# Earlier mixing, reading back and turning of token rows in four groups, and a sign strip of raw weight words moved to ScalarE

## The chip, the core and the metric

The kernel runs on one core of a Trainium2 chip. The metric is the device time of one launch in microseconds; of the kernel before, three runs are shown. The profile is one further execution of the same program, taken by the hardware profiler.

## The reference

Three stages feed each other: a causal retention layer over 4 x 576 tokens (8 heads of 64), a mixture of 8 experts of which each token uses two, and a dense layer with a gated activation. Cut to what matters:

```python
ret = (q @ k.T / 8) * Dmat          # decayed, causal; x = ret @ v, 2304 rows of 512
logits = x @ w_gate + log1p(exp(x @ w_noise)) * noise
top2, weights = two best experts of each row, softmax of the two
out[rows of e] += weight * (relu(x[rows of e] @ w1[e]) @ w2[e])      # 8 experts, 512 -> 1024 -> 512
h = out @ w_in                                                       # 512 -> 2048
y = (h * clip(h + 3, 0, 6) / 6) @ w_out                              # 2048 -> 512
```

The two matrices of the last layer arrive as 64-bit floats, and the kernel turns them into 32-bit floats itself. Each 32-bit operand of a big product is split into a high and a low part, so that every product is three passes on TensorE.

## The kernel before

The program is written out by hand: every engine (TensorE, VectorE, ScalarE, GpSimd, and the DMA queue of SyncE) works through its own list in the order in which the Python code issues it, and waits where a semaphore says so. Nothing is reordered by a scheduler.

**The expert stage** (`moe`) is ten sweeps. A sweep has eight steps f = 0 to 7, one for each 128 hidden columns. In the six middle sweeps a step has two runs of rows: 360 rows in three tiles ("ga" in PSUM) and 256 rows in two ("gb"). A step issues the first product for both runs (`g1`, L683, 12 matmuls each), the Relu and the low part of its result (L735 on ScalarE, L736 on VectorE), up to two splits of coming weights (`wstep`, L544 on ScalarE and L545 on VectorE), and then the second product of the step before (`flush`, `g2`, L694, 15 matmuls). "ga" is one PSUM buffer, so the g1 of the next step can start only when L736 has read it. Late in a sweep, `x_tile` turns the rows of the next sweep: `turn` transposes 32 x 32 blocks on VectorE (L636), copies the high part on ScalarE (L638) and takes the low part on VectorE (L639).

**The conversion of the 64-bit weights** fills the gaps of the same sweeps. There are 64 pieces of 128 x 256 words. `CV = (2, 2, 2, 1, 1, 1, 1, 1)` says how many pieces a step takes, so the first three steps of a sweep are double steps. For a piece, `cv_load` reads the raw words (SyncE), `cv_run` computes on VectorE and stores through SyncE later (`cv_store`, L594):

```python
v.tensor_scalar(a, hi, 0x7FFFFFFF, None, op0=OP.bitwise_and)      # L578, strip the sign
v.tensor_scalar(a..., min, max)                                   # L579, clamp
v.tensor_scalar(a, a, 3, 0x3FFFFFF8, shift, and)                  # L580
v.scalar_tensor_tensor(t, hi, -0x40000000, a, and, or)            # L582
v.tensor_scalar(a, t, -0x800000, None, and)                       # L583, exponent
nc.scalar.activation(lf, lo, AF.Copy, scale=2.0 ** -52)           # L585
nc.gpsimd.tensor_mul(lf, lf, a); nc.gpsimd.tensor_add(lf, t, lf)  # L586, L587
```

The tile `a` has two buffers, `lf` three; L585 waits for the store of the piece three before it.

**The dense stage** (`moe2`) works on seven groups of tiles, `GR`: three of 2 tiles, four of 3. A group has 16 steps; a step is `g1` (12 matmuls, "ga" and "gb" in turn), the gated activation (`glu`: L869, L870, L871, L872 between ScalarE and VectorE), and the `g2` of the step before. While a group runs, `x2_prep` makes the input of the next one: it gathers two rows per token from DRAM (GpSimd, L808), mixes them with the two gate weights (L816 on ScalarE, L817 on VectorE), stores the mixed rows (GpSimd's queue, L834), reads them back in blocks (SyncE, four DMAs, L628), and turns them (L636, L638, L639). It is called at the end of step f with the number f - 1, and a table of four numbers says at which number each of these happens: tile j is gathered at j * step, and mixed, read back and turned `mix`, `get` and `cut` later.

Of the kernel before, what the change touches and what calls it, by code (L numbers as in the profile page):

```python
# [7 lines left out]
F32 = mybir.dt.float32  # L8
F32R = mybir.dt.float32r
BF = mybir.dt.bfloat16  # L10
I32 = mybir.dt.int32
U32 = mybir.dt.uint32
AF = mybir.ActivationFunctionType
OP = mybir.AluOpType
# [18 lines left out]
P = 128  # L33
# [31 lines left out]
class K:  # L65
# [482 lines left out]

    def cv_init(self):
        self.cvn, self.cvl = 0, 0  # L550
        self.cvr, self.cvo = {}, []

    def cv_at(self, n, wi, wo):
        p, r = divmod(n, 8)
# [5 lines left out]
    def cv_load(self):  # L560
# [6 lines left out]
        self.nc.sync.dma_start(raw.rearrange("p f w -> p (f w)").bitcast(mybir.dt.int64), src)  # L567
        self.cvr[n] = raw

    def cv_run(self):  # L570
        n, nc, v = self.cvn, self.nc, self.nc.vector
        if not self.f64 or n >= self.cvl:
            return
        self.cvn += 1
        raw = self.cvr.pop(n)
        lo, hi = raw[:, :, 0], raw[:, :, 1]
        a = self.sb.tile([P, 256], I32, name="cva", bufs=2)
        v.tensor_scalar(a, hi, 0x7FFFFFFF, None, op0=OP.bitwise_and)  # L578
        v.tensor_scalar(a.bitcast(F32), a.bitcast(F32), fbits(0x47EFFFFF), fbits(0x38000000), op0=OP.min, op1=OP.max)  # L579
        v.tensor_scalar(a, a, 3, 0x3FFFFFF8, op0=OP.logical_shift_left, op1=OP.bitwise_and)  # L580
        t = self.sb.tile([P, 256], I32, name="cvt", bufs=2)
        v.scalar_tensor_tensor(t, hi, -0x40000000, a, op0=OP.bitwise_and, op1=OP.bitwise_or)  # L582
        v.tensor_scalar(a, t, -0x800000, None, op0=OP.bitwise_and)  # L583
        lf = self.sb.tile([P, 256], F32, name="cvl", bufs=3)
        nc.scalar.activation(lf, lo.bitcast(U32), AF.Copy, scale=2.0 ** -52)  # L585
        nc.gpsimd.tensor_mul(lf, lf, a.bitcast(F32))  # L586
        nc.gpsimd.tensor_add(lf, t.bitcast(F32), lf)  # L587
        self.cvo.append((n, lf))

# [116 lines left out]
    def moe(self, xs0):  # L706
        nc = self.nc
        xs = {(0, 0): xs0}
        self.prev = None
        for si, sw in enumerate(self.SW):  # L710
            nxt = self.SW[si + 1] if si + 1 < len(self.SW) else []
            todo = [(e, r, j) for e, r in nxt for j in range((3, 2)[r])]
            get = list(todo)
            e = sw[0][0]
            accs = None
            for f in range(8):
                n = e * 4 + f // 2
                cur = e * 4 if si in (0, len(self.SW) - 2) else n
                if f % 2 == 0:
                    if self.wsp <= cur + 4:  # L720
                        self.w_split()
                if f % 2 == 0 and (si, f) != (0, 6) or (si, f) == (0, 7):
                    self.w_load()
                self.wstep(0, n)
                if (si, f) == (0, 7):
                    for s in todo:
                        self.x_fin(*s)
                tf = 3 if si == 1 or len(todo) > 3 else 4
                w, fi = self.w[n], f % 2
                subs = []  # L730
                for q, (_, r) in enumerate(sw):
                    c = (NA, NB)[r]
                    hh, hl = self.hid([P, c]), self.hid([P, c])
                    p = self.g1(w, fi, xs[sw[q]], c, "ga" if (r == 0) == (f % 2 == 0 or len(sw) == 2) else "gb")
                    nc.scalar.activation(hh, p, AF.Relu)  # L735
                    nc.vector.scalar_tensor_tensor(hl, p, 0.0, hh.bitcast(F32), op0=OP.max, op1=OP.subtract)  # L736
                    subs.append((hh, hl, (RA, RB)[r]))
                if si == 0:
                    self.rstep()
                    self.send()  # L740
                    if f == 7:
                        for s in todo:
                            self.x_tile(s[0], xs[s[:2]], s[2], "acc", s[1])
                self.wstep()
                self.flush()
                self.wstep()
                if accs is None:
                    accs = [[self.pacc([P, DM]) for _ in range(self.run_of(*s)[1])] for s in sw]
                self.prev = (w, fi, [(*s, a) for s, a in zip(subs, accs)], f == 0, f == 7)
                self.fin = (self.y_out, sw, accs)  # L750

                if si == 0:
                    for _ in range(3):
                        self.rstep()
                        self.send()
                    if f == 4:
                        while self.sent < NT or self.live:
                            self.rstep()
                            self.send()
                        self.count()  # L760
                g = 4 if si == 0 else 0
                if f == g:
                    for s in nxt:
                        if si == 0:
                            self.x_load(*s)
                        xs[s] = self.x_new(s[1])
                    if si < 2:
                        self.fill(range(2, E) if si else range(1, 2))
                if si and get:
                    ee, rr, j = get.pop(0)  # L770
                    self.x_load(ee, rr, [j])
                sub = None
                if si and f >= tf and todo:
                    ee, rr, j = todo.pop(0)
                    sub = self.x_tile(ee, xs[ee, rr], j, r=rr)
                if si > 1:
                    for _ in range(CV[f]):
                        self.cv_run()
                        self.cv_load()
                        self.cv_store()  # L780
                elif si and f > 4:
                    self.cv_load()
                if sub:
                    sub()
                if si == len(self.SW) - 1:
                    self.x2_prep(0, f - 1)
            for s in sw:
                xs.pop(s)
# [30 lines left out]
    def x2_prep(self, gi, f):  # L819

        if gi >= len(self.GR) or f < 0:
            return
        t0, G = self.GR[gi]
        if f == 0:
            self.ys = {}
            self.x2 = (self.act_t([P, 4, 384]), self.act_t([P, 4, 384]))
        step, mix, get, cut = ((0, 2, 4, 5), (3, 5, 8, 11), (3, 5, 8, 11), (2, 5, 7, 10), (3, 3, 5, 7))[min(gi, 4)]
        for j in range(G):
            rows = self.x2d[(t0 + j) * P:(t0 + j + 1) * P]
            if f == j * step:  # L830
                self.ys[j] = self.x2_gather(t0 + j)
            if f == j * step + mix:
                self.x2_mix(t0 + j, self.ys[j])
                self.nc.gpsimd.dma_start(rows, self.ys[j][0])  # L834
            if f == j * step + get:
                self.ys[j] = self.x_blocks(rows)
            if f == j * step + cut:
                c = slice(j * P, (j + 1) * P)
                self.turn(self.ys.pop(j), slice(0, P), self.x2[0][:, :, c], self.x2[1][:, :, c])()
# [193 lines left out]
def fbits(b):  # L1033
    return float(np.array([b], np.uint32).view(np.float32)[0])
# [53 lines left out]
```

## Time and profile before

| | |
|---|---|
| three runs | 986.38, 987.69, 988.9 us; median 987.69 |
| the profiled execution, its own time | 984.52 us |
| its span, first to last instruction | 982.4 us, 16434 instructions |
| TensorE matmul / weight load busy | 960.7 us (98%) / 856.0 us (87%) |
| VectorE / ScalarE / GpSimd busy | 555.3 (57%) / 407.2 (41%) / 203.5 us (21%) |
| mean granted TensorE clock | 0.992 |
| HBM | 97.90 MB read, 39.71 MB written |

The busy share of TensorE leaves 21.7 us of the span in which it ran no matmul. Only what shortens those, or shortens the matmuls that start late because a weight load was held up, can shorten this kernel. The shares of the other engines are averages over stages that differ: the expert sweeps load VectorE far more than the dense groups do.

### The profile page before, as it was taken

To read this page: it belongs to the slowest core of one execution; us is meant where nothing else is said; L and a number is where in the kernel's file an instruction comes from. 1 tells how busy PE (TensorE), PEld (TensorE's weight loads), DVE (VectorE), ACT (ScalarE), POOL (GpSimd) and SP (SyncE) were. 2 spreads that over 40 slices of the span, in tenths; PEclk is the share of its full clock that TensorE was granted. 3 is DMA by queue.
4 is the path that set the end of the run, shared out by engine and by line. 5 is a ranking of instruction groups with operands and counts; after the bars stand their busy time and mean duration, and the time that the engine had idled before them with its cause. 6 is when DMAs were issued, how large, how long until landed. Compare 5 with 4: busy or idle time off the path is not lost.

```text
span 982.4 us, 16434 instructions
## 1 busy us (share of the span) xinstructions
PE 960.7 (98%) x6056; PEld 856.0 (87%) x6056; DVE 555.3 (57%) x1283; ACT 407.2 (41%) x844; POOL 203.5 (21%) x277
## 2 busy tenths in 40 slices
PE   8999899999999999999999999999999999999997
PEld 6888788888888889888889898989899999999996
DVE  5688745777869778786843574343434334334222
ACT  4667424444453353535342473333423333333322
POOL 1246341232314132232400211020112011020000
PEclk9999799999999999999999999999999999999999
DMA  9674747775747576584342742131223012020000
GB/s 342 236 272 168 256 149 227 238 236 166 229 165 220 187 219 188 185 252 156 90 145 70 245 162 84 36 94 43 65 65 86 33 54 76 33 86 23 33 1 36
DMA packets 106183, 138.79 MB, mean 141 GB/s; under 512 B 10469, under 2 KB 66533, under 8 KB 106093
## 3 DMA queue, kind: packets, MB, share of 16 engines
q1 hardware_dynamic: 97821, 111.03, 35.8%
q0 software_dynamic: 7984, 26.10, 7.8%
q8 instruction: 49, 0.80, 0.3%
q10 hardware_dynamic: 288, 0.52, 0.1%
q14 instruction: 41, 0.34, 0.1%
HBM read 97.90 MB, written 39.71 MB: 140 GB/s over the span
## 4 chain that ended last, share of the span: by engine, by line
PE 93%; DVE 4%; issue 1%; ACT 1%; DVEq 0%; ACTq 0%
PE p L694 41%; PE ga L683 22%; PE gb L683 20%; PE sc L192 2%; PE px L214 2%; PE p L175 2%; PE px L204 1%; DVE b L545 1%; PE p L253 1%; DVE xp L636 1%; PE p L238 1%; PE p L112 1%; PE p L272 1%; PE p L264 0%; DVE b L639 0%
## 5 line engine op out<-in xcount | busy, mean ns | idle before, releaser
L694 PE MATMUL p<-b,h 128*128 128x512 f32 (+1 forms) x1824 | 451.6, 393 | 0.0
L694 PEld LDWEIGHTS p<-b,h 128*128 128x128 f32 (+1 forms) x1824 | 330.0, 186 | 65.4 <-DVE h L736 0.3
L683 PE MATMUL ga<-x,b 128*128 128x360 f32 (+2 forms) x1344 | 236.6, 325 | 8.4 <-ACT x L638 5.4
L683 PEld LDWEIGHTS ga<-x,b 128*128 128x128 f32 x1344 | 220.6, 190 | 23.4 <-DVE h L736 8.1
L683 PE MATMUL gb<-x,b 128*128 128x384 f32 (+2 forms) x768 | 129.3, 317 | 0.0
L683 PEld LDWEIGHTS gb<-x,b 128*128 128x128 f32 x768 | 123.3, 190 | 5.2
L545 DVE TENSOR_TENSOR b<-b,b 128x512 fp32r<-128x512 f32 x128 | 93.3, 766 | 9.5 <-ACT b L544 9.3
L586 POOL TENSOR_TENSOR cvl<-cvl,cva 128x256 f32<-128x256 f32 x64 | 47.4, 740 | 241.7 <-ACT h L735 127.6
L683 PE MATMUL gb<-b,b 128*128 128x256 f32 x672 | 90.4, 283 | 0.9 <-DVE b L639 0.9
L872 DVE SCALAR_TENSOR_TENSOR h<-h,h 128x384 fp32r<-128x384 f32 (+1 forms) x112 | 56.2, 502 | 61.1 <-ACT h L871 61.1
L683 PEld LDWEIGHTS gb<-b,b 128*128 128x128 f32 x672 | 87.3, 191 | 2.6 <-DVE b L639 1.9
L871 ACT ACTIVATE h<-h 128x384 fp32r<-128x384 f32 (+1 forms) x112 | 53.7, 479 | 65.3 <-DVE h L870 65.3
L870 DVE SCALAR_TENSOR_TENSOR h<-h,ga 128x384 f32<-128x384 f32 (+1 forms) x56 | 27.8, 497 | 93.5 <-ACT h L869 93.3
L870 DVE SCALAR_TENSOR_TENSOR h<-h,gb 128x384 f32<-128x384 f32 (+1 forms) x56 | 27.8, 497 | 82.9 <-ACT h L869 82.8
L544 ACT ACTIVATE b<-b 128x512 fp32r<-128x512 f32 x128 | 73.9, 625 | 0.0
L869 ACT ACTIVATE h<-ga,three 128x384 f32<-128x384 f32 (+1 forms) x56 | 30.0, 535 | 95.5 <-PE ga L683 95.5
L736 DVE SCALAR_TENSOR_TENSOR h<-gb,h 128x256 fp32r<-128x256 f32 (+1 forms) x64 | 27.7, 433 | 70.7 <-PE p L694 48.2
L834 POOL DMA_DIRECT2D x2d<-s x18 | 10.4, 578 | 267.5 <-DVE s L817 267.4
L869 ACT ACTIVATE h<-gb,three 128x384 f32<-128x384 f32 (+1 forms) x56 | 30.0, 535 | 77.8 <-PE gb L683 77.8
L735 ACT ACTIVATE h<-gb 128x256 fp32r<-128x256 f32 (+1 forms) x64 | 25.3, 396 | 74.9 <-PE gb L683 74.9
L638 ACT ACTIVATE x<-xp 128x512 fp32r<-128x512 f32 (+1 forms) x39 | 22.8, 584 | 80.3 <-DVE xp L636 80.3
L587 POOL TENSOR_TENSOR cvl<-cvt,cvl 128x256 f32<-128x256 f32 x64 | 53.3, 832 | 5.0
(143 smaller groups left out, 891.3 us busy)
## 6 DMA issues: line engine op xcount, KB each, us to landing
b<-in_moe_w_dram SPq DMA_DIRECT2D x64, 512.0 KB, 5.2
s<-xe SPq DMA_DIRECT2D x140, 64.0 KB, 2.9
s<-in_moe_w_in_dram SPq DMA_DIRECT2D x32, 256.0 KB, 3.5
s<-in_moe_w_out_dram SPq DMA_DIRECT2D x32, 256.0 KB, 3.4
yd<-s SPq DMA_DIRECT2D x24, 240.0 KB, 2.5
b<-in_k_dram SPq DMA_DIRECT2D x18, 256.0 KB, 5.3
b<-in_q_dram SPq DMA_DIRECT2D x18, 256.0 KB, 5.4
b<-in_v_dram SPq DMA_DIRECT2D x18, 256.0 KB, 5.3
```

The lines of the kernel that those rows point to most:

```text
L544: self.nc.scalar.activation(h, a, AF.Copy)
L545: self.nc.vector.tensor_sub(l, a, h.bitcast(F32))
L586: nc.gpsimd.tensor_mul(lf, lf, a.bitcast(F32))
L587: nc.gpsimd.tensor_add(lf, t.bitcast(F32), lf)
L683: nc.tensor.matmul(p, a[:, k, f], b[:, k, :n], start=(i == 0), stop=(i == 11))
L694: nc.tensor.matmul(a[:R], x[:, c], y[:, fi, :], start=(first and i == 0), stop=(last and i == 2))
L735: nc.scalar.activation(hh, p, AF.Relu)
L736: nc.vector.scalar_tensor_tensor(hl, p, 0.0, hh.bitcast(F32), op0=OP.max, op1=OP.subtract)
L869: nc.scalar.activation(r, p, AF.Relu, bias=self.three)
L870: nc.vector.scalar_tensor_tensor(r, r, 6.0, p, op0=OP.min, op1=OP.mult)
L871: nc.scalar.activation(gh, r, AF.Copy, scale=1.0 / 6.0)
L872: nc.vector.scalar_tensor_tensor(gl, r, 1.0 / 6.0, gh.bitcast(F32), op0=OP.mult, op1=OP.subtract)
```

## The change

Two parts.

1. In the table of `x2_prep`, the rows for next groups 1 and 2 go from mix 5, get 8, cut 11 to 4, 6, 8, and the row for next group 3 from 5, 7, 10 to 4, 6, 8. The rows for group 0 and for groups 4 to 6 stay.
2. The sign strip of the raw words (L578) leaves VectorE. A new function `cv_abs` does it as an absolute value on ScalarE for the piece after the one just converted. The exponent goes to a tile of its own, `cvs`, with one buffer.

```diff
+    def cv_abs(self):
+        n = self.cvn + len(self.cva)
+        if n in self.cvr:
+            a = self.sb.tile([P, 256], I32, name="cva", bufs=2)
+            self.nc.scalar.activation(a.bitcast(F32), self.cvr[n][:, :, 1].bitcast(F32), AF.Abs)
+            self.cva.append(a)
...
-        a = self.sb.tile([P, 256], I32, name="cva", bufs=2)
-        v.tensor_scalar(a, hi, 0x7FFFFFFF, None, op0=OP.bitwise_and)
+        a = self.cva.pop(0)
...
-        v.tensor_scalar(a, t, -0x800000, None, op0=OP.bitwise_and)
+        s = self.sb.tile([P, 256], I32, name="cvs", bufs=1)
+        v.tensor_scalar(s, t, -0x800000, None, op0=OP.bitwise_and)
...
-        nc.gpsimd.tensor_mul(lf, lf, a.bitcast(F32))
+        nc.gpsimd.tensor_mul(lf, lf, s.bitcast(F32))
...
                         self.cv_run()
                         self.cv_load()
                         self.cv_store()
+                        self.cv_abs()
                 elif si and f > 4:
                     self.cv_load()
+                    if f == 7:
+                        self.cv_abs()
...
-        step, mix, get, cut = ((0, 2, 4, 5), (3, 5, 8, 11), (3, 5, 8, 11), (2, 5, 7, 10), (3, 3, 5, 7))[min(gi, 4)]
+        step, mix, get, cut = ((0, 2, 4, 5), (3, 4, 6, 8), (3, 4, 6, 8), (2, 4, 6, 8), (3, 3, 5, 7))[min(gi, 4)]
```

Where ScalarE's list changes, in a double step of an expert sweep, before (`cvl` is the tile lf, `s` the raw words, the Relus of two steps stand around it):

```order
L735 ACTIVATE h_3236<-ga 128x360
L735 ACTIVATE h_3253<-gb 128x256
L544 ACTIVATE b_3118<-b_2647 128x512
L544 ACTIVATE b_3120<-b_2649 128x512
L585 ACTIVATE cvl<-s_3114 128x256
L585 ACTIVATE cvl<-s_3219 128x256
L735 ACTIVATE h_3330<-ga 128x360
```

And the same step now (lines are 7 higher behind the new function, tile numbers shift):

```order
L742 ACTIVATE h_3251<-ga 128x360
L742 ACTIVATE h_3268<-gb 128x256
L544 ACTIVATE b_3131<-b_2653 128x512
L544 ACTIVATE b_3133<-b_2655 128x512
L592 ACTIVATE cvl<-s_3125 128x256
L574 ACTIVATE cva<-s_3231 128x256
L592 ACTIVATE cvl<-s_3231 128x256
L574 ACTIVATE cva<-s_3246 128x256
L742 ACTIVATE h_3347<-ga 128x360
```

The absolute value of the second piece of the step stands behind the copy L592 of the first one; that of the next step's first piece stands last.

ScalarE's list at the end of the first short dense group, before; `x` is the next group's input, L884 the output of the group that ends:

```order
L869 ACTIVATE h_7535<-gb,three 128x256
L871 ACTIVATE h_7520<-h_7535 128x256
L638 ACTIVATE x_7100<-xp 128x4x128
L869 ACTIVATE h_7565<-ga,three 128x256
L871 ACTIVATE h_7550<-h_7565 128x256
L884 ACTIVATE s_7576<-p_7068 128x512
```

And now:

```order
L645 ACTIVATE x_7164<-xp 128x4x128
L879 ACTIVATE h_7551<-gb,three 128x256
L881 ACTIVATE h_7536<-h_7551 128x256
L879 ACTIVATE h_7577<-ga,three 128x256
L881 ACTIVATE h_7562<-h_7577 128x256
L879 ACTIVATE h_7603<-gb,three 128x256
L881 ACTIVATE h_7588<-h_7603 128x256
L879 ACTIVATE h_7629<-ga,three 128x256
L881 ACTIVATE h_7614<-h_7629 128x256
L894 ACTIVATE s_7640<-p_7132 128x512
```

Three more activations of the old group (L879 with L881) now stand between the last turn and the first activation of the next group.

ScalarE's list in the third short group, which prepares the first group of three tiles, now; L826 is the mix (L816 before):

```order
L645 ACTIVATE x_8132<-xp 128x4x128
L826 ACTIVATE s_8249<-s_8249,gw 128x512
L879 ACTIVATE h_8392<-ga,three 128x256
L881 ACTIVATE h_8377<-h_8392 128x256
```

Here a turn and a mix fall into one step; before, each had a step of its own.

## Rows read from the trace of the kernel before

**Rows 1.** The page: the chain that ended last, by engine.

```profile
PE 93%; DVE 4%; issue 1%; ACT 1%; DVEq 0%; ACTq 0%
```

**Rows 2.** Waits of TensorE (us in total, times, longest); below, who waited for L736.

```profile
PE ga L683 <- ACT x L638: 5.4, 3, 1.8
PE ga L683 <- DVE h L736: 2.4, 1, 2.4
...
  PEld ga L683: 8.1, 19
```

**Rows 3.** Timeline, first short group's end (start us, us, engine, line, [idle before]).

```profile
602.66 0.72 DVE L636 STREAM_TRANSPOSE xp<-s 128x512 f32<-128x512 f32 x1
...
604.92 1.60 PE L683 MATMUL ga<-x,b 128*128 128x256 f32 x12
...
607.74 1.60 PE L683 MATMUL gb<-x,b 128*128 128x256 f32 x12
...
609.18 1.55 PE L694 MATMUL p<-b,h 128*128 128x512 f32 x6
...
611.89 0.60 ACT L638 ACTIVATE x<-xp 128x512 fp32r<-128x512 f32 x1 [1.13 <-DVE xp L636]
...
612.54 1.70 PE L683 MATMUL ga<-x,b 128*128 128x256 f32 x12 [1.80 <-ACT x L638]
```

**Rows 4.** Mix and store there; L834's landing; L628's issue time and landing.

```profile
593.71 0.71 ACT L816 ACTIVATE s<-s,gw 128x512 f32<-128x512 f32 x1
...
595.50 0.57 POOL L834 DMA_DIRECT2D x2d<-s  x1 [6.79 <-DVE s L817]
...
DMA to landing us min/median/max: 2.3/2.5/3.7
...
L628 SPq DMA_DIRECT2D s<-x2d x72: 302/430/593, 552.3 to 891.2; - x72
...
DMA to landing us min/median/max: 1.8/2.8/7.8
```

**Rows 5.** Timeline of the third short group, ScalarE and TensorE.

```profile
689.80 0.47 ACT L869 ACTIVATE h<-ga,three 128x256 f32<-128x256 f32 x1 [1.45 <-PE ga L683]
...
690.77 0.42 ACT L871 ACTIVATE h<-h 128x256 fp32r<-128x256 f32 x1 [0.49 <-DVE h L870]
...
692.43 1.55 PE L694 MATMUL p<-b,h 128*128 128x512 f32 x6
```

**Rows 6.** Instructions of L578 and of L585: ns, min/median/max.

```profile
L578 DVE TENSOR_SCALAR cva<-s x64: 267/280/290, 182.5 to 495.3; 128x256 int32<-128x256 int32 x64
...
L585 ACT ACTIVATE cvl<-s x64: 418/432/447, 181.8 to 495.9; 128x256 f32<-128x256 uint32 x64
```

**Rows 7.** Timeline of an expert sweep, double steps f = 1 and 2, then f = 4.

```profile
299.01 0.44 ACT L585 ACTIVATE cvl<-s 128x256 f32<-128x256 uint32 x1 [1.82 <-issue]
...
301.42 0.47 ACT L735 ACTIVATE h<-ga 128x360 fp32r<-128x360 f32 x1 [0.81 <-DVE cva L578]
...
302.82 0.29 DVE L578 TENSOR_SCALAR cva<-s 128x256 int32<-128x256 int32 x1
...
303.14 0.79 DVE L579 TENSOR_SCALAR cva<-cva 128x256 f32<-128x256 f32 x1
...
305.53 0.52 DVE L736 SCALAR_TENSOR_TENSOR h<-ga,h 128x360 fp32r<-128x360 f32 x1
...
306.11 2.23 PE L683 MATMUL ga<-x,b 128*128 128x360 f32 x12
...
320.08 2.14 PE L683 MATMUL ga<-x,b 128*128 128x360 f32 x12
```

**Rows 8.** Timeline at the start of that sweep; below, who waited for L639.

```profile
287.38 0.68 DVE L639 TENSOR_TENSOR b<-xp,b 128x512 fp32r<-128x512 f32 x1
...
288.12 0.74 PE L683 MATMUL gb<-b,b 128*128 128x256 f32 x4 [0.18 <-DVE b L639]
...
  PEld gb L683: 1.9, 5
```

More of the change, by code (lines that the diff above doesn't have):

```diff
@@ L550, in cv_init @@
         self.cvn, self.cvl = 0, 0
-        self.cvr, self.cvo = {}, []
+        self.cvr, self.cvo, self.cva = {}, [], []
     def cv_at(self, n, wi, wo):
```

## The prediction

> **What bounds the kernel now.** I read four views in this order. The chain of waits says that 93% of the span is TensorE's own work [rows 1], and the table above that it is busy 98% of it: there are 21.7 us without a matmul, part of them in stages that the change does not touch. The waits of TensorE say where the rest is [rows 2]: three waits of 1.8 us for the high part of a turned tile (L638), 5.4 us together, and a family of short ones for L736, of which the matmuls show little (one wait of 2.4 us) but the weight loads 8.1 us in 19 cases. The timeline then shows each place.
>
> The three long waits are the starts of dense groups. At the end of the first short group the last g1 starts at 607.74, the g2 of the step before at 609.18 and lasts 1.55, and then the first g1 of the next group has to wait 1.80 us, until L638 has copied the tile that was turned last [rows 3]. Nothing is missing in DRAM by then: the turn is only the last thing the table orders, at number 14 of 14, behind the whole activation of step 15.
>
> The short ones lie in the expert sweeps, at both ends. In a double step VectorE is behind by half a step; L736 ends at 306.05 and the g1 that overwrites "ga" starts at 306.11 [rows 7]. These 12 matmuls take 2.23 us where the same 12, not held up, take 2.14. At a sweep's start the low part L639 ends at 288.06 and the last four matmuls of "gb" go at 288.12 after a wait of 0.18; five such starts hold the weight loads up by 1.9 us, 0.38 each [rows 8].
>
> **The change part by part.**
>
> *Turns sooner.* No instruction is added or removed; per group 2 or 3 mixes, stores, four-fold reads and turns move. The last turn goes from number 14 to 11 (groups 1 and 2) and to 12 (group 3). A step lasts 604.92 to 607.74, 2.82 us [rows 3], so the copy is done about 8.5 or 5.6 us before the group ends, against a wait of 1.80. Is the data there? From mix to turn the new table leaves 4 steps, 11.3 us. Used are 2.4 us from L816 at 593.71 to the end of L834's issue at 596.07, 2.5 to the store's landing, 4 reads at 0.43 and 2.8 to the last one's landing [rows 4]: 9.4 us, 1.9 to spare. If both DMAs took their longest times, 3.7 and 7.8, the turn would come 4.3 us late, but that is seen once in 18 and once in 140 or fewer; VectorE and ScalarE would stand behind it. SyncE's queue waits for the store inside the reads as it did before; behind them stands only the output of the group that ends. On GpSimd's queue the third tile's gather for group 3 now stands behind the first tile's store, four steps ahead of its mix, and the stores themselves come sooner. I take the whole 5.4 us. The range is 0 (a wait of the same length at another place) to 5.7 (the first 12 matmuls took 1.70 instead of 1.60 [rows 3], three times).
>
> Against it stands one step. In the group that prepares group 3 a turn and a mix now meet. The turn alone makes ScalarE idle 1.13 us and work 0.60 [rows 3], the mix adds 0.71 [rows 4], and the next L869 had 1.45 idle before it [rows 5]: it comes 1.0 us late. From its start at 689.80 to the end of L871 at 691.19 are 1.4 us, and the g2 that needs this goes at 692.43 [rows 5], so 1.2 us cover the delay, and the low part behind it on VectorE, with the other half of the mix, may miss by a few tenths. Cost 0.2 us, once; with the extra matmul time above it cancels.
>
> *Sign strip on ScalarE, 64 pieces.* VectorE loses 64 x 0.28 = 17.9 us, ScalarE gains, by the nearest row, a copy of the same shape, 64 x 0.43 = 27.6 us [rows 6]. Neither engine bounds, so only places count.
>
> At 18 double steps (three in each of the six middle sweeps) VectorE is freed of at least 2 x 0.28 = 0.56 us before L736, more than the weight loads were held up, (8.1 - 2.4) / 18 = 0.32 [rows 2]. What TensorE gets back lies between the 0.09 of the matmul rows [rows 7] and those 0.32; the matmuls are what TensorE's time is made of, so I take 0.1, 1.8 us in all. Ends: 0, if another VectorE instruction is stretched as L579 is (0.79, against the 0.29 of L578 beside it), and 18 x 0.32 = 5.7.
>
> At five sweep starts L639 stands behind one piece and comes 0.28 us sooner, so 5 x 0.28 = 1.4 us, between 5 x 0.18 = 0.9 and 1.9 [rows 8].
>
> *What the new places wait for.* The absolute value of the second piece in a double step stands behind the first copy L585, which waited and began at 299.01; it ends by 299.01 + 0.44 + 0.43 = 299.88. VectorE wants it when the first piece is through, about where L578 stood, 302.82, less 0.28 [rows 7]: 2.7 us of lead. Behind it on ScalarE stands the Relu of the next step, at 301.42 after 0.81 idle [rows 7]; two absolute values, 0.86, may make that 0.05 late, and its reader L736 runs only at 305.53. In single steps the Relu may start up to 0.43 late while VectorE is 0.28 sooner; the result of that Relu is used one g1 and one g2 later. The raw words are needed one piece sooner, but three pieces are loaded ahead. `cvs` with one buffer makes VectorE wait for GpSimd's product of the piece before; that is one instruction, started when the exponent is ready, and three VectorE instructions of the next piece lie in between. All this I cost at nothing.
>
> The Trainium skill speaks against this part: the page "ScalarE: Activation LUTs", section "Rules for kernel authors", sends cheap elementwise work (relu, min, add, mul) to VectorE and not to ScalarE. The rows agree on the price, 0.43 against 0.28. By the rule the part would lose 64 x 0.15 = 9.7 us of engine time; by the places of rows 7 it wins, since VectorE is the late one of the two.
>
> **The sum.** 5.4 + 0 + 1.8 + 1.4 = 8.6 us. The profiled execution took 984.52, 2.1 more than its span, and would take 975.9. The median of the three runs is 987.69, 3.2 above the profiled one, so I take the same difference off it: 979.1.
>
> **The rivals.**
>
> (A) Forecast: all three terms, 979.1. Its own range, from the ends closest to the rows, 977.0 to 981.5.
>
> (B) Only the turns pay. For it: the matmuls themselves show almost no wait in the sweeps, and what is won in a double step may be lost to another stretched instruction. 987.69 - 5.4 = 982.3.
>
> (C) The turns find their data late in the short groups, so that a VectorE wait replaces TensorE's, and only the sweeps gain: 987.69 - 3.2 = 984.5. Against it: 1.9 us to spare. With neither gain it is no change, 987.7.
>
> (D) Slower: ScalarE becomes the late one, as the rule above would have it. The place is the second piece of each double step, the mechanism that its absolute value waits behind the copy L585, which itself waits for the store of an earlier piece. It decides when L585 comes more than 2.7 us later than in rows 7. If it came 4 us later, VectorE would stand 1.3, less the 0.56 saved, so 0.7 us longer before L736, and TensorE with it: 18 x 0.7 = 13 us, less 5.4 from the turns, gives 995. The trace shows ScalarE half a step ahead, so this is unlikely.
>
> (E) More: every held-up weight load is paid back in full, 5.4 + 0.3 + 5.7 + 1.9 = 13.3, 974.4.
>
> **How the numbers follow.** Chances: A 0.57, B 0.22, C 0.06, no gain 0.04, D 0.05, E 0.06. A measurement of this kernel can tell about 0.3%, 3.0 us, from no change. A, B and E are faster by more, and C at 3.2 is near the line, half counted: 0.88. Within 0.3%: 0.07. Slower: 0.05. The range leaves out D and most of E, and takes in B and C's near end with the 1.3 us by which single runs stand off their median: 975.8 to 983.6.
>
> **What would show it.** The three waits for L638 gone, and no VectorE wait for a read of x2d in their place; the windows of the short groups about 1.8 us shorter each. L578 gone, 64 absolute values of about 0.43 on ScalarE. The weight loads' wait for L736 down from 8.1 to under 4 us, the "ga" groups behind double steps at 2.14, the waits for L639 gone. The forecast is wrong if a wait for the absolute value shows on VectorE in the double steps, or if TensorE waits for L735, L736 or L872 where it did not before.

## The result, and the profile after

The changed kernel takes 977.03 us (median of four runs, 976.63 to 977.27) against 988.3 us of the kernel before (four runs, 986.38 to 989.6): a ratio of 0.9887 with a 95% interval of 0.9869 to 0.9905, so 11.3 us less, between 9.4 and 13.0. The forecast was 979.1, in a range of 975.8 to 983.6.

The page of the changed kernel: its span, the busy time of each engine, and the chain by engine [rows 1].

```profile
span 974.5 us, 16460 instructions
...
PE 955.1 (98%) x6056; PEld 855.6 (88%) x6056; DVE 535.4 (55%) x1219; ACT 427.2 (44%) x908; POOL 202.6 (21%) x277
...
PE 94%; DVE 3%; issue 1%; DMA 1%; ACT 1%; another core or an unknown queue 0%; SPq 0%; DVEq 0%; ACTq 0%
```

VectorE lost 19.9 us of work and ScalarE gained 20.0 (its 64 absolute values take 27.5, in part beside the instruction before or behind), while the span became shorter by 7.9. The totals do not tell why: TensorE idles only 2.3 us less (19.4 against 21.7) although waits of 5.4 us are gone, because the two profiled executions also differ in the first stages. The places have to be read.

TensorE's waits inside the sweeps and dense groups after the change; under it, who waited for the low part L743 (L736 before) [rows 2].

```profile
PE ga L690 <- DVE h L743: 2.4, 1, 2.4
...
  PEld ga L690: 2.8, 1
```

The three waits for the turned tile (5.4 us) are gone, and of the 19 late weight loads (8.1 us) one is left. It is the start of the third sweep, where the change does nothing. The five waits for the low part of the turn at the sweep starts [rows 8] no longer show either.

The end of the first short group, timeline (start, us, engine, line, [idle before]), to be read against [rows 3]:

```profile
600.55 0.72 DVE L643 STREAM_TRANSPOSE xp<-s 128x512 f32<-128x512 f32 x1
...
601.30 0.60 ACT L645 ACTIVATE x<-xp 128x512 fp32r<-128x512 f32 x1 [1.13 <-DVE xp L643]
...
605.63 1.60 PE L690 MATMUL gb<-x,b 128*128 128x256 f32 x12
...
607.08 1.55 PE L701 MATMUL p<-b,h 128*128 128x512 f32 x6
...
608.46 1.60 PE L690 MATMUL ga<-x,b 128*128 128x256 f32 x12
```

The copy L645 is done at 601.90, 6.6 us before the next group's first g1, which follows the last g2 by 1.38 us, as in any step. Before, that distance was 612.54 - 609.18 = 3.36. The difference is 1.98, not the 1.80 of the wait's row, because in an unbroken row each group's end lies 0.17 us behind the next one's start (607.08 + 1.55 = 608.63, and the next starts at 608.46).

The three short groups as windows, each from its first g1 to that of the next (the first pair of numbers: length, TensorE busy; near the end the granted clock):

```profile
562.58:608.46 45.88, 45.88 (x292) 41.56 (x291) 29.03 (x57) 26.87 (x58) 9.60 (x10) 1.00 0.41 133
608.46:653.69 45.23, 45.23 (x290) 41.07 (x288) 17.52 (x38) 17.50 (x39) 5.03 (x6) 1.00 0.19 59
653.69:698.88 45.19, 45.19 (x289) 40.98 (x288) 19.44 (x41) 18.59 (x41) 5.64 (x7) 1.00 0.23 71
```

And the same of the kernel before:

```profile
564.69:612.54 47.85, 46.05 (x292) 41.38 (x290) 29.07 (x58) 27.22 (x58) 9.13 (x10) 1.00 0.39 126
612.54:659.82 47.28, 45.48 (x288) 40.98 (x289) 17.62 (x39) 17.61 (x38) 6.93 (x8) 1.00 0.22 68
659.82:707.10 47.28, 45.48 (x289) 40.99 (x289) 19.61 (x42) 18.70 (x40) 3.68 (x5) 1.00 0.18 56
```

TensorE is now busy through all three; together they last 136.30 us instead of 142.41.

A double step of an expert sweep, timeline of the changed kernel [rows 7]:

```profile
299.85 0.41 ACT L574 ACTIVATE cva<-s 128x256 f32<-128x256 f32 x1
...
302.05 0.44 ACT L574 ACTIVATE cva<-s 128x256 f32<-128x256 f32 x1
...
302.33 0.29 DVE L585 TENSOR_SCALAR cva<-cva 128x256 f32<-128x256 f32 x1
302.39 0.46 ACT L742 ACTIVATE h<-ga 128x360 fp32r<-128x360 f32 x1
...
303.37 0.74 POOL L594 TENSOR_TENSOR cvl<-cvt,cvl 128x256 f32<-128x256 f32 x1
303.53 0.86 DVE L588 SCALAR_TENSOR_TENSOR cvt<-s,cva 128x256 int32<-128x256 int32 x1
...
304.71 0.53 DVE L743 SCALAR_TENSOR_TENSOR h<-ga,h 128x360 fp32r<-128x360 f32 x1
...
306.28 2.14 PE L690 MATMUL ga<-x,b 128*128 128x360 f32 x12
```

The low part L743 ends at 305.24, 1.0 us before the g1 that overwrites "ga"; before, it was 0.06. The 12 matmuls take 2.14 instead of 2.23.

The start of that sweep [rows 8]:

```profile
287.48 1.75 PE L690 MATMUL gb<-b,b 128*128 128x256 f32 x12
...
287.76 0.68 DVE L646 TENSOR_TENSOR b<-xp,b 128x512 fp32r<-128x512 f32 x1
...
289.07 3.17 PE L701 MATMUL p<-b,h 128*120 128x512 f32 x13
```

From the first "gb" matmul to the next g2 it is 1.59 us; before, 1.86.

So that kernels can be compared piece by piece, the span is cut in five: up to the first g1 of the first expert sweep; from there to the first g2 of 15 matmuls (**entry**: two sweeps and the first step of the third); from there to the first g1 of the dense groups (**sweeps**); the three **short** groups; the **tail**. us, from the start times in the timeline of every profile:

| kernel | first g1 | entry | sweeps | short | tail | span |
|---|---|---|---|---|---|---|
| before | 113.64 | 70.34 | 380.71 | 142.41 | 275.29 | 982.4 |
| before again | 116.08 | 69.90 | 380.69 | 142.47 | 275.35 | 984.5 |
| changed | 116.01 | 69.64 | 376.93 | 136.30 | 275.62 | 974.5 |
| e1 | 116.35 | 68.19 | 380.68 | 136.30 | 275.35 | 976.9 |
| e2 | 115.96 | 70.44 | 376.92 | 142.49 | 275.29 | 981.1 |
| e3 | 116.34 | 70.42 | 377.02 | 142.52 | 275.28 | 981.6 |
| e4 | 116.18 | 68.14 | 382.41 | 144.04 | 275.26 | 986.0 |
| e5 | 112.48 | 67.89 | 380.75 | 136.30 | 275.52 | 972.9 |
| e6 | 113.51 | 70.29 | 376.92 | 140.63 | 275.25 | 976.6 |
| e7 | 112.46 | 69.66 | 376.93 | 136.32 | 275.35 | 970.7 |
| e8 | 112.12 | 70.15 | 376.10 | 136.31 | 275.37 | 970.0 |
| e9 | 116.16 | 67.18 | 376.12 | 136.30 | 275.16 | 970.9 |
| e10 | 116.19 | 68.13 | 376.96 | 136.31 | 275.38 | 973.0 |

Where the same code runs, sweeps and short groups repeat to about 0.1 us and the tail to 0.5. The first two columns scatter by 4 and 2.5 us, whatever the kernel: the first went with the group of runs (116.0 to 116.4 in e1 to e4, 112.1 to 113.5 in e5 to e8, 116.1 to 116.2 in e9 to e11), the second with TensorE's clock (last section). The change is worth 3.78 us in the sweeps and 6.11 in the short groups, less 0.33 in the tail: 9.6 us, inside the interval of the timed difference.

### The profile page after: what moved, and what is told of

Read it like the earlier page. It is cut to its first block, busy times and chain, and to the rows that moved or that the text cites. A ratio compares the mean times of both kernels' runs of the same rounds, so it can differ in the third digit from the quotient of the medians.

```text
span 974.5 us, 16460 instructions
## 1 busy us (share of the span) xinstructions
PE 955.1 (98%) x6056; PEld 855.6 (88%) x6056; DVE 535.4 (55%) x1219; ACT 427.2 (44%) x908; POOL 202.6 (21%) x277
## 4 chain that ended last, share of the span: by engine, by line
PE 94%; DVE 3%; issue 1%; DMA 1%; ACT 1%; another core or an unknown queue 0%; SPq 0%; DVEq 0%; ACTq 0%
PE p L701 42%; PE ga L690 23%; PE gb L690 20%; PE sc L192 2%; PE px L214 1%; PE p L175 1%; PE px L204 1%; DVE b L545 1%; PE p L253 1%; PE p L238 1%; DMA s<-xe 1%; PE p L112 1%; DVE b L194 0%; PE p L264 0%
## 5 line engine op out<-in xcount | busy, mean ns | idle before, releaser
L690 PE MATMUL ga<-x,b 128*128 128x360 f32 (+2 forms) x1344 | 234.2, 323 | 3.0 <-DVE h L743 2.4
L593 POOL TENSOR_TENSOR cvl<-cvl,cvs 128x256 f32<-128x256 f32 x64 | 47.4, 741 | 237.4 <-ACT cva L574 197.4
L881 ACT ACTIVATE h<-h 128x384 fp32r<-128x384 f32 (+1 forms) x112 | 53.7, 479 | 66.1 <-DVE h L880 64.4
L743 DVE SCALAR_TENSOR_TENSOR h<-gb,h 128x256 fp32r<-128x256 f32 (+1 forms) x64 | 27.8, 434 | 83.9 <-PE p L701 62.2
L879 ACT ACTIVATE h<-ga,three 128x384 f32<-128x384 f32 (+1 forms) x56 | 29.9, 534 | 89.4 <-PE ga L690 89.2
L879 ACT ACTIVATE h<-gb,three 128x384 f32<-128x384 f32 (+1 forms) x56 | 30.0, 536 | 77.2 <-PE gb L690 74.7
L645 ACT ACTIVATE x<-xp 128x512 fp32r<-128x512 f32 (+1 forms) x39 | 22.8, 584 | 75.1 <-DVE xp L643 74.0
L594 POOL TENSOR_TENSOR cvl<-cvt,cvl 128x256 f32<-128x256 f32 x64 | 52.9, 827 | 5.0
```

The lines of the kernel that those rows point to most:

```text
L593: nc.gpsimd.tensor_mul(lf, lf, s.bitcast(F32))
L690: nc.tensor.matmul(p, a[:, k, f], b[:, k, :n], start=(i == 0), stop=(i == 11))
L879: nc.scalar.activation(r, p, AF.Relu, bias=self.three)
L881: nc.scalar.activation(gh, r, AF.Copy, scale=1.0 / 6.0)
```

## The experiments

They ran in three groups, each on one chip, beside the kernel before: e1 to e4 (before: 986.62 us), e5 to e8 (983.43), e9 to e11 (985.87). Ratios are to the kernel before of the same group.

**e1 and e2: each part alone.** e1 is the kernel before with the new table, e2 the changed kernel with the old table.

```diff
-        step, mix, get, cut = ((0, 2, 4, 5), (3, 5, 8, 11), (3, 5, 8, 11), (2, 5, 7, 10), (3, 3, 5, 7))[min(gi, 4)]
+        step, mix, get, cut = ((0, 2, 4, 5), (3, 4, 6, 8), (3, 4, 6, 8), (2, 4, 6, 8), (3, 3, 5, 7))[min(gi, 4)]
```

> The table of the turns alone; the sign strip stays on VectorE. Theory: the turns were only ordered too late, and the two parts do not touch each other. The three waits for L638 go, the three short groups take 136.3 us together instead of 142.2, the six two-run sweeps (first g2 after a double step to the last one, 184.1 to 504.9 in the profile of before) stay at 320.8 us: about 5.9 us faster, ratio 0.994. Rival: the turns need the freer VectorE; then a VectorE wait for the read-back or a wait of TensorE for L736 or L872 shows in the short groups and they gain less than 5 us.

> The sign strip on ScalarE a piece ahead, with the old table. Theory: VectorE is the late engine at 18 double steps (0.14 us each back) and at five sweep starts (0.27 each back): 3.9 us faster, ratio 0.996; the sweeps take 317.0 us instead of 320.8, the short groups stay at 142.2. Rival (only the turns pay): no change in the sweeps, 320.8, and the other gain of the change is the scatter of the attention stage.

Measured: e1 979.21 us, 0.9927 [0.9913, 0.9941]; e2 982.59, 0.9952 [0.9938, 0.9967]. In the table e1 has all of the gain in the short groups and none in the sweeps, e2 the reverse. 6.11 and 3.79 add up to the change's own 9.89: the parts do not touch each other. The times add up as well (7.4 + 4.0 = 11.4 us).

**e3: no sign strip at all.** It leaves the sign strip out, on either engine, so its converted weights are not the kernel's. The calls of `cv_abs` go, and the table is the old one, as in e2.

```diff
-        a = self.cva.pop(0)
-        v.tensor_scalar(a.bitcast(F32), a.bitcast(F32), fbits(0x47EFFFFF), fbits(0x38000000), op0=OP.min, op1=OP.max)
+        a = self.sb.tile([P, 256], I32, name="cva", bufs=2)
+        v.tensor_scalar(a.bitcast(F32), hi.bitcast(F32), fbits(0x47EFFFFF), fbits(0x38000000), op0=OP.min, op1=OP.max)
```

> Leaves the sign strip out: no engine does it, the clamp reads the raw words, old table. It has VectorE's relief without ScalarE's 64 instructions. Theory (ScalarE's work is hidden): the same as the strip on ScalarE alone, 3.9 us faster, sweeps 317.0 us, the difference between the two under 0.5 us. Rival (ScalarE's work costs part of the gain): at least 1 us faster than the strip on ScalarE alone.

Measured: 982.19 us, 0.9951 [0.9937, 0.9964], sweeps 377.02. That is e2 to 0.1 us: on ScalarE the strip costs nothing, and all that VectorE could give back by losing it has been given back.

**e7: the strip twice on ScalarE.** On top of the changed kernel, each absolute value is computed twice.

```diff
         a = self.sb.tile([P, 256], I32, name="cva", bufs=2)
         self.nc.scalar.activation(a.bitcast(F32), self.cvr[n][:, :, 1].bitcast(F32), AF.Abs)
+        self.nc.scalar.activation(a.bitcast(F32), self.cvr[n][:, :, 1].bitcast(F32), AF.Abs)
```

> The changed kernel with every absolute value done twice on ScalarE (the same values into the same tile): 64 more instructions, 27.5 us more ScalarE work. Theory: ScalarE's lead in the double steps and the cover in the single ones hide it; as the changed kernel within 0.5 us, ratio 0.988. Rival (ScalarE is near the bound, the slower case of the prediction): 18 double steps and up to 28 single steps show a VectorE wait for ScalarE, 3 us slower than the changed kernel or more.

Measured: 973.49 us, 0.9901 [0.9886, 0.9916]; sweeps 376.93, the changed kernel's own number. Its groups of the two lines (count, then busy us, mean ns, idle before):

```profile
L575 ACT ACTIVATE cva<-s 128x256 f32<-128x256 f32 x64 | 28.1, 439 | 2.0
L574 ACT ACTIVATE cva<-s 128x256 f32<-128x256 f32 x64 | 27.6, 431 | 15.9 <-DVE cvt L589 14.4 <-DMA s<-in_moe_w_in_dram 1.5
```

Another 28.1 us of work on ScalarE, in the very places where it would have to hurt, moved nothing. Rival D falls with this.

**e4: the absolute value in its own piece.** Not a piece ahead but just before VectorE reads it, with the old table.

```diff
-        a = self.cva.pop(0)
+        a = self.sb.tile([P, 256], I32, name="cva", bufs=2)
+        nc.scalar.activation(a.bitcast(F32), hi.bitcast(F32), AF.Abs)
```

> The strip on ScalarE, but in its own piece instead of a piece ahead, old table. Theory: in the double steps ScalarE runs half a step ahead of VectorE, so nothing is lost there (2.5 us gained); in the single steps the strip stands behind the copy of the turned tile (L638), so the clamp starts 1.2 us later, the low part L639 0.9 us later than before, and each of the five sweep starts waits 1.1 us instead of 0.2: 4.5 us lost there. Together 2 us slower than before, ratio 1.002, sweeps 322.8 us. Rival (the piece ahead is not needed): 3.9 us faster, as with the piece ahead. Rival (ScalarE becomes the late engine in the double steps): 10 us slower or more, with a VectorE wait there.

Measured: 989.4 us, 1.0031 [1.0021, 1.0041]: slower than the kernel before. Waits of TensorE in it:

```profile
PE ga L691 <- ACT x L646: 5.4, 3, 1.8
PE gb L691 <- DVE b L647: 5.0, 5, 1.0
```

The five sweep starts now wait 1.0 us each for the low part of the turn, since VectorE stands before it until ScalarE has done the absolute value. The sweeps are 1.7 us longer than before, 5.5 us longer than with the value a piece ahead; that is the part of the timed 2.8 us which has a cause in the edit. Another 1.63 us of the profile, in the short groups, is no part of the edit: one of the old 1.8 us waits was followed by matmuls at a lower clock (last section).

**e5 and e6: how much sooner a turn has to be.** e5 is the kernel before with `cut` alone one number lower; e6 the changed kernel with `cut` 7 in place of 8.

```diff
-        step, mix, get, cut = ((0, 2, 4, 5), (3, 5, 8, 11), (3, 5, 8, 11), (2, 5, 7, 10), (3, 3, 5, 7))[min(gi, 4)]
+        step, mix, get, cut = ((0, 2, 4, 5), (3, 5, 8, 10), (3, 5, 8, 10), (2, 5, 7, 9), (3, 3, 5, 7))[min(gi, 4)]
```

> The kernel before with the turns alone one step sooner in the same three rows (cut 10, 10 and 9 instead of 11, 11 and 10; mixing and reading back stay where they were). Theory: the data lie ready for some 9 us, and the last turn was only ordered too late; one step of 2.8 us against a wait of 1.8 suffices. Short groups 136.3 us instead of 142.2, as with the whole table, ratio 0.994. Rival: mixing and reading back sooner matter, or one step is not enough because the turn meets the activation; then a wait for L638 or L639 remains and the short groups take 138 us or more.

> The changed kernel with the turns one step sooner again (cut 7 instead of 8), one step behind the read-back. Theory: the slack between read and turn is used up. In groups 1 and 2 the first turn stands before the last block has landed, by about 0.9 us, and in the same step as a mix, so TensorE loses 0.8 to 1 us in each; a VectorE wait for the read of x2d shows. Group 3 has no such meeting and loses nothing. Short groups 138 us instead of 136.3, so about 2 us slower than the changed kernel, ratio to before about 0.991. Rival: the read-back has slack left; 136.3 us.

Measured: e5 977.05 us, 0.9936 [0.9923, 0.995], short groups 136.30. A step of 2.82 us is more than the 1.98 that was missing, so one number is all it takes; mix and read could have stayed. e6: 978.05 us, 0.9942 [0.9927, 0.9957], short groups 140.63: 4.3 us of the gain are lost again, 2.1, 1.6 and 0.6 in the three groups. That is more than expected (0.8 to 1 in the first two, nothing in the third). Its timeline in the first short group:

```profile
598.64 0.73 DVE L643 STREAM_TRANSPOSE xp<-s 128x512 f32<-128x512 f32 x1 [1.94 <-DMA s<-x2d]
...
600.64 0.41 DVE L880 SCALAR_TENSOR_TENSOR h<-h,ga 128x256 f32<-128x256 f32 x1
601.09 0.42 ACT L881 ACTIVATE h<-h 128x256 fp32r<-128x256 f32 x1 [0.72 <-DVE h L880]
...
601.55 1.67 PE L701 MATMUL p<-b,h 128*128 128x512 f32 x6 [1.09 <-ACT h L881]
```

VectorE waits 1.94 us for the rows read back, the activation of the running step stands behind the turn in its list, and TensorE idles at its g2. This is rival C, one step beyond the change: from mix to turn there are three steps in e6 and four in the changed kernel, and four were enough in every group.

**e8: the low part of the last turn first.** On top of the changed kernel, at a sweep's last step VectorE takes the low part before the conversion piece and not after it.

```diff
                 if si > 1:
+                    if sub and f == 7:
+                        sub()
+                        sub = None
                     for _ in range(CV[f]):
```

> The changed kernel with the low part of the last turned tile of a sweep (in step 7) ahead of the piece of the conversion instead of behind it. In the changed kernel the matmuls of gb at the five sweep starts still take 1.59 us instead of 1.43. Theory: they still wait for this low part; it comes 0.7 us sooner, and each start gains 0.16, 0.8 us in all (ratio to before 0.987), with the g1 at the starts at 1.43. Rival: VectorE's wait for the ScalarE copy before the low part only moves the conversion later, and nothing is gained or L736's successor makes the next ga wait.

Measured: 972.17 us, 0.9884 [0.9869, 0.9898]; sweeps 376.10, 0.83 us less than the changed kernel. Its sweep start, timeline of TensorE:

```profile
283.94 1.59 PE L690 MATMUL gb<-b,b 128*128 128x256 f32 x12
285.37 2.01 PE L701 MATMUL p<-b,h 128*120 128x512 f32 x8
```

From "gb" to g2 it is 1.43 us, 0.16 less than in the changed kernel, five times. The profile shows this gain; the timed ratios of two groups cannot tell it.

**e9: the entry of the third sweep.** On top of e8, the two PSUM buffers of the second sweep change places, and its turns begin a step sooner, to take away the last wait for L743.

```diff
-                tf = 3 if si == 1 or len(todo) > 3 else 4
+                tf = 2 if si == 1 else 3 if len(todo) > 3 else 4
...
-                    p = self.g1(w, fi, xs[sw[q]], c, "ga" if (r == 0) == (f % 2 == 0 or len(sw) == 2) else "gb")
+                    p = self.g1(w, fi, xs[sw[q]], c, "ga" if ((r == 0) == (f % 2 == 0 or len(sw) == 2)) != (si == 1) else "gb")
```

> This is e8_low_part_first (the changed kernel with the low part of the last turn first at sweep starts) with one more edit in the second sweep (si = 1): the two PSUM buffers of its g1 change places, so that the first g1 of the third sweep finds "ga" free, and the turns of that sweep begin one step sooner (step 2, not 3), so that the rows of the third sweep are there. In every kernel so far the profile showed one TensorE wait of 2.4 us for the low part of step 7 at this place; in four of them (before, after, e2, e8) the 12 matmuls behind it took 3.56 to 3.79 us, in two others (e1, e4) 2.26. Theory 1, the wait is the shared buffer and the slow matmuls follow from the idle time: the wait of 2.4 is gone, the 12 matmuls take 2.14, at most 0.4 us of a new wait for "gb" stands behind them: 2.0 to 3.6 us less than e8, ratio to the kernel before 0.985 to 0.986. Theory 2, the wait only moves (to the rows of the second run, whose turn was late as well, or to the first g2): the profile shows 1.5 to 2.5 us of TensorE waits at the same place and the ratio stays at 0.988. Theory 3, the slow matmuls come from elsewhere (the start of the sweep itself): no wait, but still 3.5 us for the first 12: 0.986 to 0.987.

Measured: 974.92 us (four runs, 973.14 to 976.13), 0.9895 [0.9878, 0.9911]: no gain that the times show, and the 0.985 to 0.986 of the first theory lie outside the interval. The profile, which is of the shortest of the four runs, has the wait gone, timeline of TensorE:

```profile
165.83 1.98 PE L701 MATMUL p<-b,h 128*128 128x512 f32 x6
...
172.70 1.98 PE L701 MATMUL p<-b,h 128*128 128x512 f32 x6
174.52 2.15 PE L690 MATMUL ga<-x,b 128*128 128x360 f32 x12
177.01 1.70 PE L690 MATMUL gb<-b,b 128*128 128x256 f32 x12 [0.34 <-DVE h L743]
```

The first 12 matmuls take 2.15. But the g2 of the three steps before take 1.88 to 1.98 where they took 1.55 (in e8 the last of the three 1.88), because VectorE, which begins with the turns a step sooner, is late with the low parts a step sooner: three weight loads of these g2 wait 1.4 us for L743. The entry is 67.18 us, 3.0 less than in e8, but 1.0 less than in e10, which had the wait and kept its clock. Part of the wait moved, part is gone; why the other three runs were up to 3 us longer stays open.

**e10: a third buffer for the absolute values.**

```diff
-            a = self.sb.tile([P, 256], I32, name="cva", bufs=2)
+            a = self.sb.tile([P, 256], I32, name="cva", bufs=3)
```

> The changed kernel with three buffers, not two, for the tile of the absolute values. In the changed kernel ScalarE waited 16.4 us in 14 places for VectorE to read the piece two before, which the prediction had not named. Theory 1, this wait lies beside other work, since ScalarE is ahead of VectorE in the double steps: the waits go or become a part of what they were, the stretch of the sweeps stays at 376.9 us and the ratio at 0.989. Theory 2, the wait delays the Relu of the next step and with it the "ga" buffer: the stretch of the sweeps becomes over 0.5 us shorter, ratio 0.988 or less.

Measured: 975.93 us, 0.9908 [0.9891, 0.9924]; the waits of ScalarE for L588 are gone, sweeps 376.96, as in the changed kernel. They had cost nothing.

**e11: the kernel before once more.**

> The kernel before once more, unchanged, for a second profile. Theory 1, the double steps, the short groups and the tail repeat to 0.1 us (380.7, 142.2, 275.3 us) and what differs between executions lies ahead of the first double step of the third sweep (180 to 187 us from the start, in the attention stage and in the clock behind the 2.4 us wait). Theory 2, the stretches behind it scatter as well, by 1 us or more, and then the differences between the kernels there were in part scatter.

Measured: 986.62 us. Sweeps 380.69, short groups 142.47 and tail 275.35 are within 0.06 of the first profile, as the first theory had it. Of the 2.1 us by which the spans differ, 2.0 are the start (116.08 against 113.64, with 0.44 given back in the entry).

## Why the prediction was right, step by step

- **The turns: 5.4 forecast, 6.1 measured.** The mechanism is the one named (e1, e5). The term was mis-sized: the wait's row says 1.80, but TensorE came 1.98 late, three times 5.9. The row counts from the modelled end of the last matmul, which in an unbroken row lies 0.17 behind the next start. The 0.1 us by which the first matmuls behind a wait were longer comes on top, in the second and third group (2.05 and 2.09 us shorter, against 1.97 in the first). The 8.5 us of the text are how much sooner the copy comes; its lead over the next g1 is 6.6, since TensorE is sooner too.
- **The data's 1.9 us to spare** were enough in all groups: there is no wait of a turn for its rows in the changed kernel. They were fewer than counted. With one step less (e6) VectorE waited 1.2 to 2.2 us for the rows, so of the step's 2.82 us an estimated 0.6 to 1.6 were to spare.
- **Turn and mix in one step: 0.2 forecast, 0 measured.** ScalarE and TensorE in the third short group [rows 5], timeline:

```profile
683.28 0.60 ACT L645 ACTIVATE x<-xp 128x512 fp32r<-128x512 f32 x1 [1.13 <-DVE xp L643]
...
683.77 0.71 ACT L826 ACTIVATE s<-s,gw 128x512 f32<-128x512 f32 x1
...
684.39 0.47 ACT L879 ACTIVATE h<-ga,three 128x256 f32<-128x256 f32 x1
...
685.64 0.42 ACT L881 ACTIVATE h<-h 128x256 fp32r<-128x256 f32 x1 [0.79 <-DVE h L880]
...
686.22 1.55 PE L701 MATMUL p<-b,h 128*128 128x512 f32 x6
```

  L881 ends at 686.06 and the g2 goes at 686.22, on time; 0.16 us were left of the 1.2 that covered it.
- **Double steps: 18 times 0.1 forecast, 18 times 0.13 measured** (3.78, less the starts' 1.35, is 2.43). Start by start, the 12 matmuls of "ga" give back 0.06 to 0.12 at each of the 18, 1.9 us in all, which is the term as forecast. What it left out is the first double step of a sweep, where L736 made the matmuls start late as well and not only last longer. Timeline of TensorE there, before and after:

```profile
295.57 3.63 PE L694 MATMUL p<-b,h 128*120 128x512 f32 x15
299.12 2.26 PE L683 MATMUL ga<-x,b 128*128 128x360 f32 x12
```

```profile
295.95 3.62 PE L701 MATMUL p<-b,h 128*120 128x512 f32 x15
299.41 2.14 PE L690 MATMUL ga<-x,b 128*128 128x360 f32 x12
```

  From the g2 to the g1 it was 3.55 us and is 3.46. That is 0.09 in five of the sweeps and 0.04 in the other, 0.5 us in all.
- **The lower end of that term** feared that another instruction would be stretched instead. That came true, and did no harm. Groups of VectorE's conversion lines after the change (busy us, mean ns):

```profile
L588 DVE SCALAR_TENSOR_TENSOR cvt<-s,cva 128x256 int32<-128x256 int32 x64 | 35.1, 549 | 5.7
...
L585 DVE TENSOR_SCALAR cva<-cva 128x256 f32<-128x256 f32 x64 | 17.9, 280 | 0.0
```

  and the same two of the kernel before:

```profile
L579 DVE TENSOR_SCALAR cva<-cva 128x256 f32<-128x256 f32 x64 | 27.7, 433 | 2.2
L582 DVE SCALAR_TENSOR_TENSOR cvt<-s,cva 128x256 int32<-128x256 int32 x64 | 27.3, 426 | 6.9 <-DVE cva L580 0.5
```

  The clamp is no longer stretched (9.8 us less), L588 is (7.8 more); L586 is stretched as it was before (L580). With the strip's own 17.9 VectorE is rid of 19.9 us.
- **Sweep starts: 5 times 0.28 forecast, 5 times 0.27 measured.** e8 shows that another 0.16 was to be had at each.
- **What the absolute value waits for** was incomplete. The text looked at the copy ahead of it and at its raw words. The lead that it gave the second piece, 2.7 us, was 2.1 (the value ends at 300.26, VectorE takes it at 302.33). It did not look at the value's own two buffers: ScalarE waits in 14 places for VectorE to read the piece two before.

```profile
ACT cva L574 <- DVE cvt L588: 16.4, 14, 2.0
```

  So the Relu of the next step came not 0.05 us late but 0.84 (its g1 ended at 301.55, it began at 302.39 in the timeline above). It stayed hidden because VectorE, its reader, was later still, at 304.71; e10 shows that it cost nothing.
- **The rule of the Trainium skill** ("ScalarE: Activation LUTs", "Rules for kernel authors": cheap elementwise work to VectorE) would have kept 64 x 0.15 us of engine time. The trace agrees with its price (0.43 against 0.28), but the sweeps became 3.79 us shorter by breaking it (e2), and paying the price twice cost nothing (e7). No run here shows a place where both engines are equally late.
- **The rivals.** B (only the turns) is out by e2, C by the changed kernel's own waits, D by e7 and because no VectorE wait for the absolute value shows in the changed kernel, E by e3: the sweeps give back no more when the strip is gone altogether.
- **From the sum to the time.** 9.6 us of the 11.3 have a place in the profile, 1.0 more than the sum's 8.6: 0.7 from the turns and 0.6 from the sweeps, less 0.3 in the tail. The rest, 1.7, is within the interval and no larger than the scatter of the first two columns of the table. The 8.6 lie below that interval (9.4 to 13.0); the forecast time is only 2.1 us off because the kernel before, with its fourth run, has a median 0.6 higher than the one counted from.

## What to carry to other kernels

Read the cost of a wait from start to start of the work on the late engine, not from the idle time in its row alone: here 1.80 was 1.98. An instruction is placed by which of two engines is late at that point, not by which does it cheaper, and it should stand a piece ahead of its reader; the same move made in place was slower than not moving it (e4). When a prefetch is brought forward, find out how far it may go: one step was enough (e5), three did no harm, and one step less between reading back and turning turned 4.3 us of the gain into a wait on another engine (e6).

## What the runs showed of the hardware

**The clock behind a short idle time.** At the entry of the third sweep TensorE idles 2.38 to 2.40 us in every kernel but e9. The 12 matmuls behind it took 2.25 to 2.26 us in four profiles and 3.56 to 3.79 in eight, the same code. Timelines of e1 and of the second profile of the kernel before:

```profile
175.76 2.26 PE L683 MATMUL ga<-x,b 128*128 128x360 f32 x12 [2.40 <-DVE h L736]
```

```profile
176.28 3.65 PE L683 MATMUL ga<-x,b 128*128 128x360 f32 x12 [2.39 <-DVE h L736]
```

In the second the granted clock is 0.93 over the 26 us from 160 to 186, in the first 1.00, so these matmuls ran at 1.2 GHz for a good part and not at 2.4. The outcome went along with something 60 us earlier: in the four profiles that kept the clock, the first 12 matmuls of the expert stage took 3.54 to 3.78 us and the next 12 2.14 or 2.15; in the other eight 3.97 and 2.67 to 3.22. From the g2 before the idle time to the g2 behind both g1 it is 8.08 or 8.09 us in the four and 8.91 to 9.14 in the eight, so the lower clock cost 0.8 to 1.1 us: of what the four won at these 12 matmuls they lost a part again, in a wait of 0.21 us ahead of the next 12. No edit here set the outcome; its cause stays open. With the clock at the start of the stage it accounts for the entry column of the table (67.9 to 68.2 against 69.6 to 70.4). e4 had the same behind one of its 1.8 us waits, the only one of 15 in five profiles (the two of the kernel before, e2, e3, e4), where the granted clock over the next 2.5 us was 0.54:

```profile
614.58 2.83 PE L691 MATMUL ga<-x,b 128*128 128x256 f32 x12 [1.80 <-ACT x L646]
```

In the kernel before these took 1.70 [rows 3]. Taking out a short idle time can therefore have a second value that one profile need not show.

**Two engines at the same memory.** L588, with two inputs in SBUF, took 0.43 us alone and 0.86 beside GpSimd's L594 (303.53 and 303.37 in the double step above). The Trainium skill ("SBUF — State Buffer", "Who interferes with whom") says that a VectorE instruction with two such inputs contends with a GpSimd instruction that reads SBUF. The trace agrees on that. It shows more: the clamp and the shift behind it (L580 before, L586 after) have one input each, of which that sentence says nothing, and took 0.79 beside GpSimd's instructions and 0.29 alone. The stretch moved: the two conversion instructions that stood beside GpSimd's product and sum were the long ones, the clamp and the shift before the change, the shift and L588 after it.
